# Last combinations in one-bank tiles with copies by block, another place for two steps of the tail, and last logits by blocks

## The chip, the cores and the metric

The kernel runs on one core of one Trainium2 chip. The metric is the device time of one execution in microseconds, lower is better; a time quoted without more is the median of the runs that are not profiled. All data is fp32.

## The reference

A gated linear attention feeds a soft mixture of experts. Cut to what matters:

```python
# q, k, v, f_logit: batch 4, heads 8, 768 tokens, head size 48
f = 1 / (1 + exp(-f_logit))
for t in range(S):
    state = f[:, :, t, :, None] * state + einsum('bhd,bhe->bhde', k[:, :, t], v[:, :, t])
    y[:, :, t] = einsum('bhd,bhde->bhe', q[:, :, t], state)
x = y.transpose(0, 2, 1, 3).reshape(3072, 384)

logits = x @ phi                                   # 3072 tokens x 32 slots (8 experts x 4)
d = softmax of logits over the tokens (axis 0)
slot_input = d.T @ x                               # 32 x 384
slot_out[e] = relu(slot_input[e] @ w1[e]) @ w2[e]  # 384 -> 1024 -> 384, 8 experts
c = softmax of logits over the slots (axis 1)
out = c @ slot_out                                 # 3072 x 384
```

The softmax over the tokens needs the logits of all tokens, so no expert can start before the last token's logits are there; and no output row can be made before the experts are done.

## The kernel before

The attention is done in 12 units of work (`NU`; half of the batch rows times 128 tokens), the mixture in 6 groups of two units (`NV`). Each unit goes through decays (ScalarE, VectorE, GpSimd), scores, mask, and the inner products that make y in transposed form in the PSUM tiles PB[0] and PB[1] (`intra`, L283). ScalarE copies y to SBUF (`y_copy`, L294), TensorE transposes it back (`x_tr`, L299). Once both units of a group have their y, `c_lg` (L317) makes the group's logits, 32 slots x 128 columns for each of four blocks n: blocks 0 and 1 take the group's first unit, blocks 2 and 3 the second, one block for each y copy. A block is 32 columns of TensorE wide and sums over four chunks p. `c_max` keeps a running maximum over the tokens, `c_exp`, `c_tr`, `c_copy` bring the exponentials to the other layout, `c_pin` (L360) pools x with them and `c_join` adds that to the sum with rescaling.

The last group (units 10 and 11) is the bottleneck's end: its logits lie in PC[:, 0], a column behind them (L327, `c_first`) holds the old maximum, so that one reduction (L331) gives the new one. From it a chain of small steps (`t_max`, `c_exp`, `c_pin`, `t_psi`) leads to the pooled inputs of the experts, and `tail` begins: `up` (L423, first weights, ScalarE relu), `turn` (L429, transposes, with a masked VectorE copy L430), `down` (L469, second weights). `down` runs in two parts of the 384 output columns, h = 0 with 256 and h = 1 with 128 columns, 16 steps of four matmuls each. `slot_out` (L476, VectorE) scales the result, `slot_out2` (L481 TensorE, L482 ScalarE's copy to s4) sums it over the experts' copies.

Then come the combinations, `combine(h, y)`, three for each h: combination weights ct times s4 for two groups of tokens. `c_ct(h)` (L463 transposes, L465 copy) brings these weights, softmaxed over the slots, into ct, for h = 0 the first three groups, for h = 1 the last three. A combination makes 8 matmuls L501 in four banks of PSUM, one for each block n of 32 partitions of s4, two groups x each; the copies to SBUF (stage) are ScalarE's L503, for the two banks of a pair at once, and VectorE's L509 (`combine_2`), one for each of the other two. `store` (L513) sends the result out: 1 MB for h = 0, 0.5 MB for h = 1. All stores are issued on SyncE's queue but the last, which ScalarE issues.

PSUM has eight banks here: four single tiles PA[0], PA[1], PB[0], PB[1], and two pairs, PC and PD, each one tile of two banks. The tile layer puts in the semaphore waits, and each engine works in the order in which the program is written. That order comes from a table: `at(t, fn, ...)` gives each step a time in units of T, `run_atoms` sorts by it, and `tail` and `last` are lists written out by hand at the end. The step that the change to `at` touches reads:

```python
    at((NU - 1) * T + 6.1, c_first, NV - 1)
```

In the rows, tile names come in small letters (pa, pb, pc, pd for PA to PD, s for s4, wr also for the stage of the output), and an fp32 matmul is two passes, so 16 products show as x32.

Of the kernel before, what the change touches and what calls it, by code (L numbers as in the profile page):

```python
# [16 lines left out]
NU = 12  # L17
NV = 6
# [5 lines left out]
WC, CO = (256, 128), (0, 256)  # L24
# [20 lines left out]
T = 8.6  # L45
# [12 lines left out]
def gla_soft_moe_kernel(ctx: ExitStack, tc: tile.TileContext, q, k, f, v, vd, phi, w1, w2, out):  # L58
# [9 lines left out]
    nc = tc.nc  # L68
# [3 lines left out]
    def P(shape, name, dt=F32):  # L72
        return pool.tile(shape, dt, tag=name, name=name)
# [6 lines left out]
    def at(t, fn, *args):  # L80
        atoms.append((round(t, 4), len(atoms), fn, args))
# [38 lines left out]
    pin = P([128, DM], "pin")  # L120
# [17 lines left out]
    PA, PB = ([pp.tile([128, 512], F32, tag=f"{n}{w}", name=f"{n}{w}") for w in range(2)] for n in ("pa", "pb"))  # L138
    PC, PD = (pp.tile([128, 2, 512], F32, tag=n, name=n) for n in ("pc", "pd"))
# [168 lines left out]
    def lgs(g):  # L308
        return PA[0][:, :128] if g < NV - 1 else PC[:, 0, :128]
# [1 line left out]
    def trs(g):  # L311
        return PB[0] if g < NV - 2 else PC[:, 1]

    def c_lg(g):
        for p in range(4):
            for n in range(4):
                nc.tensor.matmul(lgs(g)[32 * n : 32 * n + 32], phs[:, p], xTs[2 * g + n // 2][:, n % 2, p], start=p == 0, stop=p == 3)  # L317


# [158 lines left out]
    def slot_out2(h):  # L478
# [4 lines left out]


    FIN = [
        [(PC, PA[0], PA[1]), (PD, PB[1], PA[0]), (PC, PA[1], PB[1])], [(PD, PB[0], PA[1]), (PC, PB[1], PA[0]), (PD, PB[0], PA[1])],
    ]
    stage = [
        wr[:, a:b].rearrange("p a x -> p (a x)").rearrange("p (v n d) -> p v n d", v=NV, n=4) for a, b in ((7, 11), (11, 13))
    ]  # L490

    def combine(h, y, last=(2, 3)):

        hs_, wc = slice(CO[h], CO[h] + WC[h]), WC[h]
        two, b2, b3 = FIN[h][y]
        banks = [two[:, 0], two[:, 1], b2, b3]
        for n2 in range(2):
            for x in range(2):
                for n in (n2, n2 + 2):
                    ns = slice(32 * n, 32 * n + 32)  # L500
                    nc.tensor.matmul(banks[n][:, wc * x : wc * x + wc], ct[ns, 2 * y + x], s4[ns, hs_], start=True, stop=True)  # L501
        dst = stage[h][:, 2 * y : 2 * y + 2]
        nc.scalar.copy(dst[:, :, :2].rearrange("p v n d -> p n v d"), two[:, :, : 2 * wc].rearrange("p n (v d) -> p n v d", v=2))  # L503
        for n in last:
            combine_2(h, y, n)

    def combine_2(h, y, n):
        wc = WC[h]
        nc.vector.tensor_copy(stage[h][:, 2 * y : 2 * y + 2, n], FIN[h][y][n - 1][:, : 2 * wc].rearrange("p (v d) -> p v d", v=2))  # L509

    def store(h, y):
        o, n = 4 * NV * CO[h], 8 * WC[h]
# [35 lines left out]
    STEPS = [(j, kk) for j in range(2) for kk in range(8)]  # L548

    def tail(late):  # L550

        items = [(t_psi,), (c_exp, NV - 1, (1,)), (t_zs,), (up, 0, 0), (up, 0, 1), (up, 1, 0)]
        items += [(c_tr, NV - 1, (1,)), (flag_2,), (c_copy, NV - 1, (1,)), (turn, 0, 0), (turn, 0, 1), (t_z,), (c_soft, 1), (flag_3,), (c_soft2, 1), (up, 1, 1)]
        items += [(load_w2, i, home) for i, home in late]
        items += [(down, 0, *STEPS[x]) for x in range(8)]
        items += [(turn, 1, 0), (turn, 1, 1), (c_ct, 1)]
        items += [(down, 0, *STEPS[x]) for x in range(8, 16)]
        items += [(slot_out, 0)]
        items += [(down, 1, *STEPS[x]) for x in range(3)]
        items += [(slot_out2, 0)]  # L560
        items += [(down, 1, *STEPS[x]) for x in range(3, 7)]
        for y in range(3):
            items += [(combine, 0, y, (2,) if y == 2 else (2, 3))]
            items += [(store, 0, y)] if y < 2 else []
            items += [(down, 1, *STEPS[x]) for x in ((7, 8, 9), (10, 11, 12), (13, 14, 15))[y]]
        items += [(slot_out, 1), (combine_2, 0, 2, 3), (store, 0, 2), (slot_out2, 1), (hint,)]
        for y in range(3):
            items += [(combine, 1, y), (store, 1, y)]
        return items


    o = OFF
# [55 lines left out]
    at((NU - 1) * T + 6.5, flag)  # L628
    at((NU - 2) * T + 6.45, c_soft, 0)
    at((NU - 1) * T + 6.4, c_soft2, 0)  # L630
    at((NU - 1) * T + 6.1, c_first, NV - 1)

    for i in range(16):
        at((1.6 + 0.62 * i) * T - 0.9, load_w1, i)
# [1 line left out]
    def span(name, n=1):  # L636
        off = place[name][0]
        return [arena[:, off + UN * x : off + UN * x + UN] for x in range(n)]

    homes = list(zip(  # L640
        [9 * T + 6.9, 10 * T + 6.9, 10 * T + 4.5, 10 * T + 4.6, 10 * T + 4.0, 11 * T + 4.0, 10 * T + 6.4, 11 * T + 6.4, 12 * T - 0.5],
        span("f", 2) + span("p", 2) + span("k", 2) + span("q", 2) + span("v"),
    ))
    homes.sort(key=lambda a: a[0])
    for i, (t, home) in enumerate(homes):
        at(t, load_w2, i, home)
    spare = span("xT")[0]
# [4 lines left out]
    ending = tail(late)  # L652
    z = NU * T - 0.4
    last = [
        (x_tr, NU - 1, (0,)), (c_lg, NV - 1), (x_tr, NU - 1, (1,)), (load_w2, len(homes) - 1, spare), (x_copy, NU - 1, (0,)), (c_max, NV - 1),
        (t_max,), (c_exp, NV - 1, (0,)), (x_copy, NU - 1, (1,)), (c_tr, NV - 1, (0,)), (c_ct, 0, (0,)), (t_max2,), (c_copy, NV - 1, (0,)), (t_max3,),
        (c_pin, NV - 1), (c_ct, 0, (1,)), (c_join, NV - 1), (warm, 1),
    ]
# [126 lines left out]
```

## Time and profile before

| | us |
|---|---|
| median of 3 runs without profile | 156.45 (156.2 to 156.59) |
| the profiled execution | 155.44 |
| its span, first to last instruction | 153.7 |
| TensorE matmul busy | 138.1 (90%) |
| VectorE, ScalarE, GpSimd busy | 104.3, 94.3, 58.5 |
| DMA | 53.97 MB, mean 351 GB/s over the span |

TensorE is busy nearly all the time up to 140 us. A busy share says little about the tail, though: there the last row of TensorE ends about 9 us before the span does, and the rest is the stores on their way. So the time line around 104 to 112 us (the last group's logits) and 128 to 146 us (the combinations), the issue times of the stores and the DMA share by slices are what is to be read.

### The profile page before, as it was taken

The page shows a single profiled execution, that of the slowest core. Times are in us where ns is not written, and L with a number is a line of the kernel's source. Part 1 is how long each engine was busy: PE and PEld are TensorE (multiplying, and loading weights), DVE is VectorE, ACT ScalarE, POOL GpSimd, SP SyncE. Part 2 cuts the span into 40 slices and gives each one's busy share as a digit, 9 for nine tenths or more (in the row PEclk, how much of TensorE's full clock was granted, in tenths as well). Part 3 has the DMA queues.
Part 4 walks back from the last instruction along what each step waited for, and adds up shares of the span by engine and source line. Part 5 has one row for each costly group of instructions (what it writes and reads, how often), then busy time and mean ns, then how long its engine had stood idle before and what let it go on. Part 6 is the DMA issues. An engine that isn't in the chain of part 4 may idle for free.

```text
span 153.7 us, 5505 instructions
## 1 busy us (share of the span) xinstructions
PE 138.1 (90%) x2392; PEld 109.4 (71%) x2392; DVE 104.3 (68%) x153; ACT 94.3 (61%) x182; POOL 58.5 (38%) x51
## 2 busy tenths in 40 slices
PE   7987999999889999999999999999889999997500
PEld 7976888989769898889879897877433556675400
DVE  6899686999579887896969887759510563146500
ACT  4998899997789796969596976334402121035400
POOL 7008585788556483909293655600000000000000
PEclk9999999999999999999999999999999999999965
DMA  4899999999999999999999939999999993009990
GB/s 153 279 364 421 402 408 406 412 409 411 410 404 415 401 410 398 393 401 389 397 410 406 388 113 374 412 419 420 417 417 337 422 422 156 0 4 420 409 386 32
DMA packets 13424, 53.97 MB, mean 351 GB/s; under 512 B 1488, under 2 KB 1616, under 8 KB 13008
## 3 DMA queue, kind: packets, MB, share of 16 engines
q1 hardware_dynamic: 13248, 53.02, 87.2%
q10 hardware_dynamic: 144, 0.52, 0.9%
q8 instruction: 20, 0.33, 0.9%
q14 instruction: 12, 0.10, 0.2%
HBM read 48.82 MB, written 4.72 MB: 348 GB/s over the span
## 4 chain that ended last, share of the span: by engine, by line


## 5 line engine op out<-in xcount | busy, mean ns | idle before, releaser
L210 POOL TENSOR_TENSOR arena<-arena 128x512 f32<-128x512 f32 (+1 forms) x15 | 28.6, 1908 | 38.9 <-ACT arena L196 28.4
L239 DVE TENSOR_TENSOR arena<-pd,mask 128x1024 f32<-128x1024 f32 x23 | 27.8, 1210 | 10.2 <-PE pd L230 10.2
L193 DVE TENSOR_TENSOR_SCAN arena<-again,arena 128x512 f32<-128x512 f32 (+1 forms) x17 | 30.3, 1787 | 3.3 <-ACT arena L188 3.3
L230 PE MATMUL pd<-arena 48*128 48x128 f32 x368 | 27.0, 285 | 1.6 <-DVE arena L239 0.6
L206 POOL TENSOR_TENSOR arena<-arena 128x512 f32<-128x512 f32 (+1 forms) x15 | 27.6, 1852 | 0.4 <-POOL arena L206 0.4
L230 PEld LDWEIGHTS pd<-arena 48*128 48x128 f32 x368 | 22.3, 187 | 5.7 <-POOL arena L206 1.7
L283 PE MATMUL pb<-arena 128*48 128x128 f32 x384 | 23.5, 274 | 0.0
L283 PEld LDWEIGHTS pb<-arena 128*48 128x48 f32 x384 | 20.3, 123 | 1.1 <-issue 0.8
L196 ACT ACTIVATE arena<-arena 128x512 f32<-128x512 f32 (+1 forms) x17 | 13.6, 801 | 10.5 <-DVE arena L193 10.5
L294 ACT COPY arena<-pb 128x512 f32<-128x512 f32 x24 | 13.6, 584 | 6.6 <-PE pb L283 6.3
L185 ACT ACTIVATE arena<-arena 128x512 f32<-128x512 f32 (+1 forms) x16 | 13.5, 847 | 1.5 <-DMA arena<-in_f_dram 1.5
L202 ACT ACTIVATE arena<-arena 128x512 f32<-128x512 f32 (+1 forms) x17 | 13.8, 811 | 0.3
L188 ACT ACTIVATE arena<-arena 128x512 f32<-128x512 f32 (+1 forms) x16 | 13.5, 844 | 0.5
L299 PE MATMUL pa<-ident,arena 112*128 112x112 f32 x96 | 11.6, 262 | 0.3 <-ACT arena L294 0.3
L274 PE MATMUL pb<-arena 48*48 48x128 f32 x320 | 10.9, 274 | 0.0
L299 PEld LDWEIGHTS pa<-ident,arena 112*128 112x128 f32 x96 | 9.7, 141 | 1.1 <-ACT arena L294 0.7
L252 PE MATMUL pc<-arena 128*48 128x48 f32 x320 | 9.2, 210 | 0.9 <-ACT arena L222 0.9
L252 PEld LDWEIGHTS pc<-arena 128*48 128x48 f32 x320 | 8.1, 125 | 2.6 <-ACT arena L222 1.1
L219 PE MATMUL pc<-ident,arena 112*128 112x112 f32 x80 | 9.9, 266 | 0.0
L274 PEld LDWEIGHTS pb<-arena 48*48 48x48 f32 x320 | 8.4, 119 | 1.4 <-issue 0.2
L219 PEld LDWEIGHTS pc<-ident,arena 112*128 112x128 f32 x80 | 7.8, 141 | 1.9 <-issue 1.0
L165 PE MATMUL pd<-ones 128*128 128x128 f32 x50 | 7.3, 317 | 1.1 <-POOL ones L143 1.1
(140 smaller groups left out, 199.3 us busy)
## 6 DMA issues: line engine op xcount, KB each, us to landing
wr<-in_w_dram SPq DMA_DIRECT2D x22, 768.0 KB, 8.6
arena<-in_w_dram SPq DMA_DIRECT2D x10, 768.0 KB, 9.4
arena<-in_f_dram SPq DMA_DIRECT2D x10, 512.0 KB, 7.4
arena<-in_q_dram SPq DMA_DIRECT2D x10, 512.0 KB, 8.5
arena<-in_k_dram SPq DMA_DIRECT2D x10, 512.0 KB, 7.1
arena<-in_v_dram SPq DMA_DIRECT2D x12, 384.0 KB, 7.3
out_dram<-wr SPq DMA_DIRECT2D x3, 1024.0 KB, 4.8
arena<-in_f_dram SPq DMA_DIRECT2D x4, 256.0 KB, 4.1
```

Of the source, the lines that this page charges most:

```text
L193: nc.vector.tensor_tensor_scan(t, cols(again, h), t, 0.0, op0=ALU.mult, op1=ALU.add)
L196: nc.scalar.activation(cols(R("p", u), h), cols(R("f", u), h), AF.Exp, scale=-1.0)
L202: nc.scalar.activation(cols(G(u), h), cols(R("f", u), h), AF.Exp)
L206: (eng or nc.gpsimd).tensor_tensor(t, t, cols(G(u), h), op=ALU.mult)
L210: (eng or nc.gpsimd).tensor_tensor(t, t, cols(R("p", u), h), op=ALU.mult)
L219: nc.tensor.transpose(PC[:, a // 4, 128 * (a % 4) : 128 * (a % 4) + W], kq[:W, a], ident[:W, :W])
L230: nc.tensor.matmul(t[:, 128 * p : 128 * p + 128], kq[rs, 4 * w + p], qq[rs, 4 * w + p], start=True, stop=True)
L239: nc.vector.tensor_tensor(dst, src, mask.unsqueeze(1).broadcast_to(list(dst.shape)), op=ALU.mult)
L252: nc.tensor.matmul(kvs[64 * r : 64 * r + D, a], kr[:, a, r], vb(u, a, r ^ a // 4), start=True, stop=True)
L274: nc.tensor.matmul(ys[a][o : o + D], heads(S0(u), D)[rs, a], qq[rs, a], start=p == 0, stop=False, skip_group_check=True,)
L283: nc.tensor.matmul(ys[4 * w + p][o : o + D], vb(u, 4 * w + p, r ^ w), sc[:, r, p], start=u < 2 and p == 0, stop=p == 3, skip_group_check=True,
L299: nc.tensor.transpose(PA[w][:, 128 * p : 128 * p + W], xTs[u][:W, w, p], ident[:W, :W])
```

## The change

Four things. The last group's logits are made in two calls of `c_lg`: blocks 0 and 1 (unit 10) behind the pooling of the group before, blocks 2 and 3 (unit 11) where all four stood; `c_first` moves one unit ahead. In `FIN` a combination's four banks are listed one by one, and none takes both banks of PC or PD; the copies go bank by bank, ScalarE blocks 0 and 1, VectorE blocks 2 and 3, in the order 0, 2, 1, 3 (the line is now L503 for both engines, and a store's is L509). `c_ct(1)` stands behind `slot_out(0)` instead of behind the turns. And the combinations of h = 0 stand elsewhere among the steps of `down(1)`: the first behind 2 steps instead of 7, the second behind 7 instead of 10, the third behind all 16 and `slot_out(1)` instead of behind 13.

```diff
-    def c_lg(g):
+    def c_lg(g, blocks=(0, 1, 2, 3)):
         for p in range(4):
-            for n in range(4):
+            for n in blocks:
                 nc.tensor.matmul(lgs(g)[32 * n : 32 * n + 32], phs[:, p], xTs[2 * g + n // 2][:, n % 2, p], start=p == 0, stop=p == 3)

     FIN = [
-        [(PC, PA[0], PA[1]), (PD, PB[1], PA[0]), (PC, PA[1], PB[1])], [(PD, PB[0], PA[1]), (PC, PB[1], PA[0]), (PD, PB[0], PA[1])],
+        [(PC[:, 0], PA[1], PB[1], PD[:, 0]), (PA[0], PC[:, 1], PD[:, 1], PB[1]), (PA[1], PC[:, 0], PD[:, 0], PB[1])],
+        [(PC[:, 1], PA[0], PB[0], PD[:, 1]), (PA[1], PC[:, 0], PB[1], PD[:, 0]), (PA[0], PC[:, 1], PB[0], PD[:, 1])],
     ]
...
-        dst = stage[h][:, 2 * y : 2 * y + 2]
-        nc.scalar.copy(dst[:, :, :2].rearrange("p v n d -> p n v d"), two[:, :, : 2 * wc].rearrange("p n (v d) -> p n v d", v=2))
-        for n in last:
-            combine_2(h, y, n)
-
-    def combine_2(h, y, n):
-        wc = WC[h]
-        nc.vector.tensor_copy(stage[h][:, 2 * y : 2 * y + 2, n], FIN[h][y][n - 1][:, : 2 * wc].rearrange("p (v d) -> p v d", v=2))
+        for n in (0, 2, 1, 3):
+            (nc.scalar.copy if n < 2 else nc.vector.tensor_copy)(
+                stage[h][:, 2 * y : 2 * y + 2, n], banks[n][:, : 2 * wc].rearrange("p (v d) -> p v d", v=2),
+            )
...
-        items += [(turn, 1, 0), (turn, 1, 1), (c_ct, 1)]
+        items += [(turn, 1, 0), (turn, 1, 1)]
         items += [(down, 0, *STEPS[x]) for x in range(8, 16)]
-        items += [(slot_out, 0)]
-        items += [(down, 1, *STEPS[x]) for x in range(3)]
-        items += [(slot_out2, 0)]
-        items += [(down, 1, *STEPS[x]) for x in range(3, 7)]
-        for y in range(3):
-            items += [(combine, 0, y, (2,) if y == 2 else (2, 3))]
-            items += [(store, 0, y)] if y < 2 else []
-            items += [(down, 1, *STEPS[x]) for x in ((7, 8, 9), (10, 11, 12), (13, 14, 15))[y]]
-        items += [(slot_out, 1), (combine_2, 0, 2, 3), (store, 0, 2), (slot_out2, 1), (hint,)]
+        items += [(slot_out, 0), (c_ct, 1), (slot_out2, 0)]
+        items += [(down, 1, *STEPS[x]) for x in range(2)]
+        items += [(combine, 0, 0), (store, 0, 0)]
+        items += [(down, 1, *STEPS[x]) for x in range(2, 7)]
+        items += [(combine, 0, 1), (store, 0, 1)]
+        items += [(down, 1, *STEPS[x]) for x in range(7, 16)]
+        items += [(slot_out, 1), (combine, 0, 2), (slot_out2, 1), (store, 0, 2), (hint,)]
...
-    at((NU - 1) * T + 6.1, c_first, NV - 1)
+    at((NU - 1) * T + o["pin"] - 3 * T + 0.01, c_lg, NV - 1, (0, 1))
+    at((2 * NV - 3) * T + o["mx"] + 0.01, c_first, NV - 1)
...
-        (x_tr, NU - 1, (0,)), (c_lg, NV - 1), (x_tr, NU - 1, (1,)), (load_w2, len(homes) - 1, spare), (x_copy, NU - 1, (0,)), (c_max, NV - 1),
+        (x_tr, NU - 1, (0,)), (c_lg, NV - 1, (2, 3)), (x_tr, NU - 1, (1,)), (load_w2, len(homes) - 1, spare), (x_copy, NU - 1, (0,)), (c_max, NV - 1),
```

What that does to the engines' order shows at three places. The first is TensorE around the last logits (L230 scores, L360 pooling of the group before, L283 inner products of the last unit, L299 its transposes; pa_85, pa_86 are PA[0], PA[1], pb_87, pb_88 are PB[0], PB[1]):

```order
 L230 MATMUL pd<-arena 128x128 x8
 L360 MATMUL pa_86<-arena,el 32x384 x4
-L283 MATMUL pb_87<-arena 48x128 x8
-L283 MATMUL pb_88<-arena 48x128 x8
-L299 MATMUL pa_85<-ident,arena 128x112 x4
-L317 MATMUL pc<-arena,phs 32x128 x16
+L317 MATMUL pc<-arena,phs 32x128 x8
+L283 MATMUL pb_87<-arena 48x128 x8
+L283 MATMUL pb_88<-arena 48x128 x8
+L299 MATMUL pa_85<-ident,arena 128x112 x4
+L317 MATMUL pc<-arena,phs 32x128 x8
```

Eight of the sixteen products went ahead of the inner products; the other eight stayed behind the first transposes.

The second is TensorE from the sum of h = 0 to the second combination, in the changed program, with the semaphores that an instruction waits for (a wait on DVE is one for VectorE, on Activation one for ScalarE):

```order
L501 MATMUL pc<-s_84,ct 128x256 [waits Activation_49]
L501 MATMUL pb_88<-s_84,ct 128x256
L501 MATMUL pc<-s_84,ct 128x256
L501 MATMUL pb_88<-s_84,ct 128x256
L501 MATMUL pa_86<-s_84,ct 128x256
L501 MATMUL pd<-s_84,ct 128x256
L501 MATMUL pa_86<-s_84,ct 128x256
L501 MATMUL pd<-s_84,ct 128x256
L469 MATMUL pb_87<-arena 32x128 x20
L501 MATMUL pa_85<-s_84,ct 128x256
L501 MATMUL pd<-s_84,ct 128x256 [waits DVE_49]
```

The second combination starts 20 products behind the first, and its second instruction, into PD, waits for VectorE once more after the first combination's last product into PD.

The third is ScalarE from the first combination to the copy of the second sum (L482), before and after:

```order
L482 COPY s_84<-pd 128x256
L503 COPY wr<-pc 128x2x2x256
L503 COPY wr<-pd 128x2x2x256
L503 COPY wr<-pc 128x2x2x256
L482 COPY s_84<-pa_85 128x128
```

```order
L482 COPY s_84<-pd 128x256
L503 COPY wr<-pc 128x2x256
L503 COPY wr<-pa_86 128x2x256
L503 COPY wr<-pa_85 128x2x256
L503 COPY wr<-pc 128x2x256
L503 COPY wr<-pa_86 128x2x256
L503 COPY wr<-pc 128x2x256
L482 COPY s_84<-pa_85 128x128
```

Each copy of two banks became two of one bank, and the copy of the second sum still stands behind those of the third combination, which on TensorE now comes after all of `down(1)`.

## Rows read from the trace of the kernel before

**Rows 1.** The page's first line.

```profile
span 153.7 us, 5505 instructions
```

**Rows 2.** Time line, last logits: start us, us, engine line op out<-in xcount [idle before<-releaser].

```profile
103.58 0.85 PE L360 MATMUL pa<-arena,el 128*32 128x384 f32 x8
...
104.36 1.95 PE L283 MATMUL pb<-arena 128*48 128x128 f32 x32
...
106.25 0.60 PE L299 MATMUL pa<-ident,arena 112*128 112x112 f32 x4
106.37 0.58 ACT L294 COPY arena<-pb 128x512 f32<-128x512 f32 x1 [0.29 <-PE pb L283]
...
106.78 1.29 PE L317 MATMUL pc<-arena,phs 128*32 128x128 f32 x32
...
108.11 0.29 DVE L331 TENSOR_REDUCE nmx<-pc 128x1 f32<-128x129 f32 x1 [0.39 <-PE pc L317]
```

**Rows 3.** Time line, TensorE: an earlier group's logits and what follows them.

```profile
95.73 1.06 PE L317 MATMUL pa<-arena,phs 128*32 128x128 f32 x32
...
96.72 1.95 PE L283 MATMUL pb<-arena 128*48 128x128 f32 x32
```

**Rows 4.** Time line: first up product; then windows: stretch, us, busy by engine, PEclk, DMA.

```profile
112.27 2.78 PE L423 MATMUL pa<-wr,et 128*32 128x512 f32 x24 [0.39 <-DVE et L413]
...
112.50:120.00 7.50, 7.50 (x72) 2.08 (x64) 0.00 (x0) 1.19 (x2) 0.00 (x0) 1.00 0.98 376
```

**Rows 5.** Time line around the second turn of the combine weights.

```profile
128.35 0.69 DVE L430 TENSOR_TENSOR arena<-pb,emask 128x512 f32<-128x512 f32 x1 [2.51 <-PE pb L429]
...
128.59 0.49 PE L463 MATMUL pa<-ident,el 128*128 128x128 f32 x3
...
129.10 0.11 PEld L469 LDWEIGHTS pd<-arena 128*32 128x32 f32 x2 [0.26 <-DVE arena L430]
```

**Rows 6.** Time line: first two combinations; the first row is a pair of single-bank copies on ScalarE.

```profile
99.61 1.05 ACT L294 COPY arena<-pb 128x512 f32<-128x512 f32 x2
...
134.00 1.08 PE L469 MATMUL pb<-arena 128*32 128x128 f32 x32
134.10 0.37 ACT L482 COPY s<-pd 128x256 f32<-128x256 f32 x1 [4.51 <-PE pd L481]
...
135.01 0.48 PE L501 MATMUL pc<-s,ct 32*128 32x256 f32 x1
...
136.19 1.29 DVE L509 COPY wr<-pa 128x512 f32<-128x512 f32 x2 [2.88 <-PE pa L501]
...
136.26 1.01 ACT L503 COPY wr<-pc 128x1024 f32<-128x1024 f32 x1 [1.79 <-PE pa L501]
...
136.89 0.48 PE L501 MATMUL pd<-s,ct 32*128 32x256 f32 x1
...
137.99 0.30 PE L469 MATMUL pb<-arena 128*32 128x128 f32 x2
```

**Rows 7.** Time line, issues of the first three stores (SyncE) and the last (ScalarE).

```profile
137.54 0.35 SPq L513 DMA_DIRECT2D out_dram<-wr  x1
...
139.42 0.34 SPq L513 DMA_DIRECT2D out_dram<-wr  x1
...
141.82 0.33 SPq L513 DMA_DIRECT2D out_dram<-wr  x1
...
145.12 0.38 ACTq L513 DMA_DIRECT2D out_dram<-wr  x1
```

**Rows 8.** Windows of the store traffic: the last two columns are DMA share and GB/s.

```profile
138.30:138.40 0.10, 0.10 (x14) 0.10 (x8) 0.10 (x1) 0.10 (x1) 0.00 (x0) 1.00 0.81 328
...
138.50:149.75 11.25, 4.80 (x106) 3.43 (x94) 4.67 (x11) 3.59 (x6) 0.00 (x0) 0.90 1.00 404
149.75:150.25 0.50, 0.00 (x0) 0.00 (x0) 0.00 (x0) 0.00 (x0) 0.00 (x0) 0.50 0.29 115
...
151.00:151.75 0.75, 0.00 (x0) 0.00 (x0) 0.00 (x0) 0.00 (x0) 0.00 (x0) 0.50 0.05 22
```

More of the change, by code (lines that the diff above doesn't have):

```diff
@@ L490, in gla_soft_moe_kernel, with combine @@
     ]
-    def combine(h, y, last=(2, 3)):
+    def combine(h, y):
         hs_, wc = slice(CO[h], CO[h] + WC[h]), WC[h]
-        two, b2, b3 = FIN[h][y]
-        banks = [two[:, 0], two[:, 1], b2, b3]
+        banks = FIN[h][y]
         for n2 in range(2):
```

## The prediction

> **What bounds the kernel now.** I read the time line of the two stretches that the change touches, then the issue times of the stores, then the DMA share of the last 16 us in slices. The profiled execution took 155.44 us, of which the span from first to last instruction is 153.7 [rows 1]; 1.74 us lie around it. The median of the runs without a profile is 156.45, 1.01 us above. I work out a difference against the profiled execution and add it to the median.
>
> Three things set the end, one after the other. First, TensorE around 104 to 108 us: the second-last group's pooling (L360) is followed without a pause by the last unit's inner products (L283, 104.36, 1.95 us), the transposes (L299, 106.25) and the last logits (L317, 106.78) [rows 2]. VectorE's maximum (L331, 108.11) waits for the logits, and a chain of small steps leads from it to the up products, which wait 0.39 us for its last step at 112.27 and then keep TensorE busy for every microsecond of 112.5 to 120 [rows 2, 4]. From there TensorE goes on without slack: whatever delays the maximum delays the first store. Second, the first store: it is issued at 137.54 and its data begins in the slice 138.30 to 138.40, so 0.8 us later [rows 7, 8]. Third, the store traffic: from 138.5 to 149.75 the 16 DMA engines are busy all the time at 404 GB/s, then most stop, and a few go on until about 151.7 [rows 8]. The six stores carry 4.72 MB, and 4.72 MB at 404 GB/s is 11.7 us. So the end is the start of the first store's data plus a fixed amount of traffic, as long as no later store comes too late.
>
> **Part 1, last logits by blocks.** The 16 products of the last group are cut in two: blocks 0 and 1 (unit 10) now stand ahead of the last unit's inner products, and only blocks 2 and 3 (unit 11) stay at 106.78. The cost hangs on how TensorE runs four blocks of 32 columns. An earlier group's 32 passes take 1.06 us at 273 ns each, so eight run at once on average counting their latency, and the next kind of product starts 0.99 us after the first pass [rows 3]. That is eight rounds of four passes: (1.06 - 0.27) / 7 = 0.11 us a round. The four blocks run side by side, and each has eight passes of its own (four chunks, two passes for each fp32 product). Two blocks therefore also take eight rounds, 8 x 0.11 = 0.88 us.
>
> What does it save at 106.78? Block 3 needs the second copy of unit 11, which ends at 106.37 + 0.58 = 106.95; its eight rounds from there end at 106.95 + 0.05 + 7 x 0.11 + 0.27 = 108.04, which is when the row of L317 ends (106.78 + 1.29 = 108.07) [rows 2]. So block 3 alone sets the end of the logits, and taking blocks 0 and 1 away saves nothing there. What does it cost at 104.3? TensorE has no pause there: L360's row ends at 104.43, L283's begins at 104.36 and ends at 106.31, L299's begins at 106.25 [rows 2]. The early half pushes all of that back. Bounds: 0 if it ran beside its neighbours, 0.99 by the earlier group's row; I take 0.87, since it follows products of the same width and so adds no second change of shape. The stopgap column of the maximum (L327, 0.15 us on VectorE) also moves forward, ahead of work that VectorE finishes before TensorE needs it, and is costed at nothing; if that cover were gone it would cost 0.15.
>
> **Part 2, the second turn of the combine weights** (three transposes L463 and ScalarE's copy L465). Before, it stood ahead of the second half of the down products. Those wait for VectorE's masked copy (128.35 + 0.69 = 129.04) and start at 129.10 with 0.26 us idle after the turn [rows 5], so the turn was hidden and taking it away gains nothing. Its new place is after the last down product of the first part, while VectorE scales the result; 0.49 us fit into that stretch, which 12 products of the next part filled before. TensorE's sum still waits for VectorE and comes at the same time; ScalarE's copy (about 0.48 us) is over before the sum's copy at 134.10 is due [rows 6]. Cost zero.
>
> **Part 3, first combination earlier.** 28 down products of the second part stood ahead of it; now there are 8. Its input is ready at 134.10 + 0.37 = 134.47. Before, 16 products ran from 134.00 and it started at 135.01; with 8 of them, four rounds of 0.11 fewer, it starts at 134.57. Everything behind it comes 0.43 to 0.44 us earlier. Its copies: VectorE still has two of 512 columns, 1.29 us together; ScalarE's one copy of 1024 (1.01) becomes two of 512, which take 1.05 together at 99.61 [rows 6]. VectorE ends last as before, so copies by block neither help nor hurt the first store. It is issued at 137.54 - 0.43 = 137.11 on the old clock (all times of parts 3 and 4 leave out part 1's shift).
>
> **Part 4, what comes behind.** Second combination: TensorE reaches it after 20 products at 136.89, as before [rows 6]. But in the changed program's order its product into the second bank of PD waits for VectorE, and the only thing of PD that VectorE still has to read is the first combination's copy out of the first bank, which is VectorE's second and ends at 135.76 + 1.29 = 137.05. So it starts at 137.10, 0.21 late; queued behind it on TensorE are the rest of the combination and nine steps of down products, and the second store waits for it: 139.42 + 0.21 = 139.63. In the Trainium skill, "PSUM — Partial Sum Buffer", section "PSUM bank collisions raise a hardware error", different banks may be read and written at once; by that the wait would not be needed and the 0.21 would be gone, but no run here shows it, and the program has the wait.
>
> Third combination: it now stands behind all nine steps (18 rounds of 0.11) instead of three. From 137.99 + 0.21: down products to about 140.2, combination from 140.3, copies from 141.5 to 142.8, store issued at 142.85, against 141.82 before [rows 7]: 1.03 us later. ScalarE's copy of the second sum now queues behind two copies of this combination and ends near 142.9, so the last three stores are issued 0.9 to 1.6 us later, the last at about 146.7 instead of 145.12 [rows 7].
>
> Does the traffic notice? Two stores of 1.05 MB at 404 GB/s last 5.19 us: from 137.92 to 143.11. The third store's data can begin 0.8 us after its issue, at 143.65 to 143.70. The engines then pause for 0.55 us. The last three stores are issued at least 0.9 us before the traffic reaches them and cost nothing. For an engine that keeps up, the sum of the tail is -0.43 + 0.57 = +0.14. For the few that lag at the end, and whose end is the end [rows 8], the pause is partly or wholly filled by the work they are behind with: down to -0.43. I take -0.1, between the two, nearer to the engines that keep up at that moment. In the Trainium skill, "DMA: Bandwidth & Descriptors", section "Latency and other measured facts", the first byte comes after about 600 ns. The rows here show 0.8; by the page the pause would be 0.2 shorter and the tail some 0.1 to 0.2 better.
>
> **Sum.** +0.87 - 0.1 = +0.77 us: 156.2 in a profile, and 156.45 + 0.77 = 157.2 as a median.
>
> **Rivals.** (A) The lagging engines swallow the pause, so the tail gives its full 0.43: +0.87 - 0.43 = +0.44, 156.9. For it: the drip after 149.75 is long, 1.9 us [rows 8]. Against it: most of that lag seems to arise in the second half of the traffic. (B) The early half of the logits costs nothing, because TensorE runs it in columns that its neighbours leave idle; then the tail alone counts: -0.1, 156.35, or -0.43 with A, 156.0. This decides once the early half costs less than 0.57. Against it: the inner products before and after fill both halves of the columns, and TensorE has no pause from 103.6 on. (C) The pause is longer: if the wait on PD holds back more than 0.21, or the copies of the third combination, now on both engines while the sum's copy waits, take 0.3 more, the third store's data begins at 144.0 and no engine can fill the pause: +0.87 + 0.14 + 0.3 = +1.3, 157.75.
>
> **How the numbers follow.** About 0.3%, 0.47 us, is what a measurement of this kernel can tell from no change: 155.98 to 156.92. Forecast 0.52, A 0.2, B 0.08, C 0.2. The forecast's own spread is 156.95 to 157.5. Faster needs B with the whole tail: 0.04. Same: the rest of B, more than half of A, and the low edge of the forecast: 0.22. Slower: 0.74. The range reaches from the lower part of A to C: 156.5 to 157.75, leaving out B and the far side of C.
>
> **What would show it.** Right: the last unit's inner products start near 105.2 instead of 104.36, the maximum near 109.0, the up products near 113.1, the first store is issued near 138.0 (0.4 later than before, not 0.9), the third near 143.7, and the DMA share has a dip of about half a microsecond near 144. Wrong: inner products that still start by 104.5 (B), no dip (A), a dip over 0.8 us (C), or a last logits row much shorter than 1.1 us, which would say that the number of blocks does count.

## The result and the profile after

The changed kernel takes 157.49 us (157.38 to 157.62), the kernel before 156.32 (156.04 to 156.59) beside it: ratio 1.0075, 95% interval 1.0054 to 1.0096, so 1.17 us slower. The prediction was 157.2 in a range of 156.5 to 157.75. In a later comparison the changed kernel came to 1.0064 (1.0036 to 1.0093).

The profiled execution took 157.62 us, against 155.44 before; its page begins:

```profile
span 155.9 us, 5511 instructions
```

Of those 2.2 us, 0.66 lie ahead of everything that the change touches: the pooling of the second-last group (L360) begins at 104.24 instead of 103.58, and one of the first loads lands that much later too (the fifth, at 8.62 instead of 7.97). The pooling's start moves from run to run, between 103.6 and 104.7 over all profiles below. So stages are compared from the pooling on, not from zero.

**The head.** The time line of the changed kernel around the last logits, to be read against [rows 2] (start us, us, engine, line, operation, count, idle before):

```profile
104.24 0.85 PE L360 MATMUL pa<-arena,el 128*32 128x384 f32 x8
...
104.91 1.04 PE L317 MATMUL pc<-arena,phs 128*32 128x128 f32 x16
...
105.88 1.96 PE L283 MATMUL pb<-arena 128*48 128x128 f32 x32
...
108.30 1.29 PE L317 MATMUL pc<-arena,phs 128*32 128x128 f32 x16
...
109.62 0.29 DVE L331 TENSOR_REDUCE nmx<-pc 128x1 f32<-128x129 f32 x1 [1.31 <-PE pc L317]
```

The inner products (L283) start 1.64 us behind the pooling's start instead of 0.78. The second half of the logits, with half the products, takes the same 1.29 us as all of them did. So the maximum stands 5.39 us (5.386 before the rows are rounded) behind the pooling's start instead of 4.53: 0.86 lost, and nothing saved.

**The first store.** From the maximum on, the path is the one of before; this is its time line around the first two combinations, with the stores' issues (SPq, ACTq), to be read against [rows 5 to 7]:

```profile
134.20 0.55 PE L463 MATMUL pa<-ident,el 128*128 128x128 f32 x3
134.34 0.48 DVE L476 TENSOR_SCALAR sob<-pd,small 128x256 f32<-128x256 f32 x1 [3.19 <-PE pd L469]
134.79 0.48 ACT L465 COPY ct<-pa 128x384 f32<-128x384 f32 x1 [8.33 <-PE pa L463]
...
134.88 0.70 PE L481 MATMUL pd<-sob,same 128*128 128x256 f32 x2
...
135.62 0.37 ACT L482 COPY s<-pd 128x256 f32<-128x256 f32 x1 [0.35 <-PE pd L481]
...
136.08 0.48 PE L501 MATMUL pc<-s,ct 32*128 32x256 f32 x1
136.09 0.48 PE L501 MATMUL pb<-s,ct 32*128 32x256 f32 x1
136.11 0.48 PE L501 MATMUL pa<-s,ct 32*128 32x256 f32 x1
136.12 0.48 PE L501 MATMUL pd<-s,ct 32*128 32x256 f32 x1
...
137.90 0.68 DVE L503 COPY wr<-pd 128x512 f32<-128x512 f32 x1
...
138.40 0.48 PE L501 MATMUL pa<-s,ct 32*128 32x256 f32 x1
138.63 0.48 PE L501 MATMUL pd<-s,ct 32*128 32x256 f32 x1
...
138.64 0.35 SPq L509 DMA_DIRECT2D out_dram<-wr  x1
...
141.15 0.34 SPq L509 DMA_DIRECT2D out_dram<-wr  x1
...
144.38 0.33 SPq L509 DMA_DIRECT2D out_dram<-wr  x1
...
148.34 0.38 ACTq L509 DMA_DIRECT2D out_dram<-wr  x1
```

The first store is issued 29.02 us behind the maximum (138.64 - 109.62) instead of 29.43: 0.41 gained. The second combination's product into PD waits to 138.63, just behind VectorE's copy out of PD's other bank (137.90 + 0.68 = 138.58), and the second store comes 2.51 us behind the first instead of 1.88. The third comes 5.74 behind it instead of 4.28.

**The traffic.** Windows of the changed kernel (stretch, us, busy by engine, TensorE clock, DMA share, GB/s), to be read against [rows 8]:

```profile
138.60:139.50 0.90, 0.90 (x16) 0.79 (x15) 0.00 (x0) 0.00 (x0) 0.00 (x0) 1.00 0.00 0
139.50:144.25 4.75, 3.90 (x97) 2.96 (x90) 2.86 (x5) 2.32 (x5) 0.00 (x0) 1.00 1.03 416
144.25:144.50 0.25, 0.22 (x5) 0.22 (x9) 0.07 (x1) 0.00 (x0) 0.00 (x0) 1.00 0.86 360
144.50:145.25 0.75, 0.75 (x24) 0.75 (x20) 0.18 (x1) 0.23 (x1) 0.00 (x0) 1.00 0.25 98
145.25:151.50 6.25, 2.32 (x28) 1.62 (x24) 2.08 (x6) 1.72 (x6) 0.00 (x0) 0.73 1.00 397
151.50:152.25 0.75, 0.00 (x0) 0.00 (x0) 0.00 (x0) 0.00 (x0) 0.00 (x0) 0.50 0.51 175
```

The data of two stores is through at 144.25, the third store's data begins 0.87 us behind its issue at 144.38, and in between the engines lose 0.25 x 0.14 + 0.75 x 0.75 = 0.60 us. Data start 139.50, 11.7 us of traffic and 0.60 of pause end at 151.8, which is where the share falls.

This dip is a low reading: the share of 1.03 ahead of it counts packets whole that run into it, and it is a mean over all engines, of which one may work on through it. The landings tell it more sharply. Each store lands (reports that its data has arrived) in 16 parts, whose times the trace has. The middle ones (the median of the 16), counted from the first issue:

| store | 1 | 2 | 3 | 4 | 5 | 6 | last part of all |
|---|---|---|---|---|---|---|---|
| kernel before | 3.81 | 6.30 | 8.81 | 10.11 | 11.41 | 12.67 | 14.57 |
| changed kernel | 3.83 | 6.31 | 9.54 | 10.83 | 12.12 | 13.42 | 15.65 |

From the third store on the middle parts are 0.71 to 0.75 later and stay so. The last part of all comes about 2 us behind the middle ones in both kernels.

### The profile page after: what moved, and what is told of

Read it like the earlier page. It is cut to its first block, busy times and chain, and to the rows that moved or that the text cites. A ratio compares the mean times of both kernels' runs of the same rounds, so it can differ in the third digit from the quotient of the medians.

```text
span 155.9 us, 5511 instructions
## 1 busy us (share of the span) xinstructions
PE 140.6 (90%) x2392; PEld 111.7 (72%) x2392; DVE 104.3 (67%) x153; ACT 94.8 (61%) x188; POOL 58.4 (37%) x51
## 4 chain that ended last, share of the span: by engine, by line
PE 64%; DVE 11%; DMA 9%; ACT 4%; issue 3%; SPq 2%; POOL 2%; POOLq 0%; DVEq 0%; ACTq 0%
PE pd L230 11%; PE pb L283 8%; DMA arena<-in_q_dram 5%; PE pd L469 5%; PE pb L274 5%; PE pa L299 4%; DVE arena L193 4%; DMA arena<-in_f_dram 4%; PE pc L219 4%; PE pc L252 4%; PE pa L423 3%; PE pb L423 3%; PE pa L360 3%; PE pb L469 3%; PE pa L317 2%
## 5 line engine op out<-in xcount | busy, mean ns | idle before, releaser
L230 PE MATMUL pd<-arena 48*128 48x128 f32 x368 | 27.0, 285 | 1.4 <-DVE arena L239 0.8
L230 PEld LDWEIGHTS pd<-arena 48*128 48x128 f32 x368 | 22.3, 187 | 5.5 <-DVE arena L239 1.8
L283 PE MATMUL pb<-arena 128*48 128x128 f32 x384 | 23.5, 274 | 0.0
L283 PEld LDWEIGHTS pb<-arena 128*48 128x48 f32 x384 | 20.3, 123 | 0.6 <-issue 0.4
L299 PE MATMUL pa<-ident,arena 112*128 112x112 f32 x96 | 11.6, 262 | 0.3 <-ACT arena L294 0.3
L299 PEld LDWEIGHTS pa<-ident,arena 112*128 112x128 f32 x96 | 9.7, 141 | 1.1 <-ACT arena L294 0.7
```

The source lines that it names most:

```text
L230: nc.tensor.matmul(t[:, 128 * p : 128 * p + 128], kq[rs, 4 * w + p], qq[rs, 4 * w + p], start=True, stop=True)
L283: nc.tensor.matmul(ys[4 * w + p][o : o + D], vb(u, 4 * w + p, r ^ w), sc[:, r, p], start=u < 2 and p == 0, stop=p == 3, skip_group_check=True,
L299: nc.tensor.transpose(PA[w][:, 128 * p : 128 * p + W], xTs[u][:W, w, p], ident[:W, :W])
```

## The experiments

Each kernel was timed beside the kernel before. The table has the ratio with its interval, and from each profile the stages: pooling's start to maximum, maximum to first issue, first issue to the end of the span, and what the DMA share lost before the last store's data began (from windows, as above). Spans are printed to 0.1 us, so the column "to the end" holds to 0.05. A row's name is the heading of its section below.

| kernel | ratio | pooling to maximum | to first issue | to the end | dip |
|---|---|---|---|---|---|
| before | 1 | 4.53 | 29.43 | 16.16 | 0 |
| changed | 1.0075 (1.0054 to 1.0096) | 5.39 | 29.02 | 17.26 | 0.60 |
| changed, again | 1.0064 (1.0036 to 1.0093) | 5.39 | 29.03 | 16.97 | 0.65 |
| whole logits | 1.0019 (0.9996 to 1.0042) | 4.53 | 29.02 | 16.91 | 0.56 |
| split alone | 1.0095 (1.0057 to 1.0133) | 5.39 | 29.44 | 16.98 | 0 |
| split alone, again | 1.0091 (1.0058 to 1.0124) | 5.39 | 29.43 | 16.18 | 0 |
| one block early | 1.0110 (1.0056 to 1.0164) | 5.38 | 29.43 | 16.19 | 0 |
| pair banks | 1.0089 (1.0060 to 1.0119) | 5.39 | 28.99 | 17.13 | 0.41 |
| third early | 0.9992 (0.9968 to 1.0017) | 4.53 | 29.02 | 16.25 | 0.30 |
| third early, pair banks | 0.9975 (0.9945 to 1.0004) | 4.53 | 29.00 | 16.40 | 0 |
| first store in halves | 0.9959 (0.9933 to 0.9985) | 4.53 | 28.47 | 16.58 | 0.41 |
| halves, second form | 0.9961 (0.9938 to 0.9984) | 4.53 | 28.47 | 16.51 | 0.32 |

The theory at the start: the early half of the logits costs 0.86 us because TensorE has no pause there (H), the earlier first combination gives back 0.41, and the pause ahead of the third store costs its length again (P). The rivals: the head's delay is absorbed (B), or a lagging DMA engine fills the pause, so that it costs nothing (L).

### Whole logits

```diff
-    at((NU - 1) * T + o["pin"] - 3 * T + 0.01, c_lg, NV - 1, (0, 1))
-    at((2 * NV - 3) * T + o["mx"] + 0.01, c_first, NV - 1)
+    at((NU - 1) * T + 6.1, c_first, NV - 1)
...
-        (x_tr, NU - 1, (0,)), (c_lg, NV - 1, (2, 3)), (x_tr, NU - 1, (1,)), (load_w2, len(homes) - 1, spare), (x_copy, NU - 1, (0,)), (c_max, NV - 1),
+        (x_tr, NU - 1, (0,)), (c_lg, NV - 1), (x_tr, NU - 1, (1,)), (load_w2, len(homes) - 1, spare), (x_copy, NU - 1, (0,)), (c_max, NV - 1),
```

> The changed kernel with one part undone: the last group's logits stand whole in their old place again, all 16 products behind the first transposes of the last unit, and the column for the maximum in its old place. Theory H (the early half of the logits delays the inner products by its whole length, and block 3 alone sets the end of the logits): inner products start some 0.8 us after the pooling instead of 1.64, maximum, first store and end 0.86 us earlier, so 157.49 - 0.86 = 156.6 (156.4 to 156.85). What is left over the kernel before (156.32) is then the tail's share, +0.3. Rival B (the head is absorbed before the stores, and the whole difference comes from the tail): 157.3 to 157.5, while the maximum comes earlier.

Measured 156.33, a ratio of 1.0019 against 1.0075 and 1.0064 for the changed kernel: 0.7 to 0.9 us of the loss are gone. The 156.33 lies just under the expected 156.4 to 156.85, but the kernel before took 156.04 beside it instead of 156.32; the ratio is the expected one. In its time line everything is back:

```profile
104.04 0.85 PE L360 MATMUL pa<-arena,el 128*32 128x384 f32 x8
...
104.83 1.96 PE L283 MATMUL pb<-arena 128*48 128x128 f32 x32
...
107.24 1.29 PE L317 MATMUL pc<-arena,phs 128*32 128x128 f32 x32
108.57 0.29 DVE L331 TENSOR_REDUCE nmx<-pc 128x1 f32<-128x129 f32 x1 [0.39 <-PE pc L317]
```

The maximum stands 4.53 us behind the pooling's start, as before. B falls. What remains over the kernel before is the tail: 0.41 earlier at the first issue, 0.75 longer from there.

### Split alone, and again

To the kernel before, only the lines of the last diff the other way round, with `c_lg` taking its blocks.

> The kernel before with one part of the change alone: the last logits in two halves, and the column for the maximum moved with them; combinations, copies and the turn of the weights as before. Theory H: maximum and first store 0.86 us later, and nothing behind them reacts, so 156.32 + 0.86 = 157.2 (156.95 to 157.4). Rival B (absorbed): 156.2 to 156.5. If it comes out above 157.4, the later start meets something else in the store traffic.

> The kernel before with the split logits alone, run again, since its first comparison (1.0095, interval 1.0057 to 1.0133, six runs) lies above the 0.86 us that its trace shows between pooling and maximum. Theory H: 1.0055 (0.86 us), with 14.6 us from the first store's issue to the last landing as in the kernel before. Rival: a late start of the tail costs another 0.5 us behind the last landing, ratio 1.009 again.

The time line of the second run:

```profile
103.61 0.85 PE L360 MATMUL pa<-arena,el 128*32 128x384 f32 x8
...
105.25 1.95 PE L283 MATMUL pb<-arena 128*48 128x128 f32 x32
...
108.99 0.29 DVE L331 TENSOR_REDUCE nmx<-pc 128x1 f32<-128x129 f32 x1 [1.31 <-PE pc L317]
```

The traces say H to the hundredth: maximum 5.39 behind the pooling's start, everything up to the last landing as before (14.68 and 14.57 us behind the first issue, 14.57 in the kernel before), and in the second run, whose pooling starts at the same time as that of [rows 2] (103.61 and 103.58), a profiled execution of 156.32 against 155.44. But the runs without a profile say 1.0095 and 1.0091, 1.4 to 1.5 us, with the lower ends of the intervals at 0.9; the first median, 157.70, is above the expected 157.4. In the first run's profile 0.7 us of excess can be seen: the span ends 2.3 us behind the last store's landing instead of 1.6, with a late fetch of instructions in between. The second shows none of it. Some may lie ahead of the pooling: it starts at 104.21 in the mean of the six profiles with split logits and at 103.84 in that of the six without; whether that is the split or scatter was not tested. So H's price is shown by the traces and by the kernel with whole logits; why the runs without a profile of this kernel lie another half microsecond higher stays open, and by medians alone the parts do not add up (1.4 for the split, 0.3 for the tail, 1.0 to 1.2 for both).

### One block early

To the kernel with the split alone:

```diff
-    at((NU - 1) * T + o["pin"] - 3 * T + 0.01, c_lg, NV - 1, (0, 1))
+    at((NU - 1) * T + o["pin"] - 3 * T + 0.01, c_lg, NV - 1, (0,))
```

and `(1, 2, 3)` instead of `(2, 3)` for the call that stays behind.

> The kernel before, with only block 0 of the last group's logits in the early place instead of blocks 0 and 1 (4 products instead of 8), and blocks 1 to 3 at the old place. If TensorE's time goes by rounds and the blocks run side by side, one block costs as much as two: inner products 0.86 us later than in the kernel before (1.64 us behind the pooling's start), the maximum too, time 156.04 + 0.86 = 156.9. If it goes by products, half: inner products 1.21 us behind the pooling's start, maximum 0.43 later, 156.5.

Its time line around the last logits:

```profile
104.70 0.85 PE L360 MATMUL pa<-arena,el 128*32 128x384 f32 x8
105.37 1.04 PE L317 MATMUL pc<-arena,phs 128*32 128x128 f32 x8
106.33 1.96 PE L283 MATMUL pb<-arena 128*48 128x128 f32 x32
...
108.75 1.29 PE L317 MATMUL pc<-arena,phs 128*32 128x128 f32 x24
```

Four products in one block of columns hold the inner products back as long as eight in two (0.96 us from L317's start to L283's; 0.97 above), so what is paid for here is rounds, not blocks. The 12 that stay take 1.29 us like 16, but there block 3, whose y copy is the last to come, sets the end. Its median, from four runs, 158.06 against an expected 156.9, is high like that of the split alone.

### Pair banks

```diff
-        [(PC[:, 0], PA[1], PB[1], PD[:, 0]), (PA[0], PC[:, 1], PD[:, 1], PB[1]), (PA[1], PC[:, 0], PD[:, 0], PB[1])],
+        [(PC[:, 0], PC[:, 1], PA[0], PA[1]), (PD[:, 0], PD[:, 1], PB[1], PA[0]), (PC[:, 0], PC[:, 1], PA[1], PB[1])],
...
```

> The changed kernel with the list of banks of the kernel before: blocks 0 and 1 of a combination in both banks of PC or of PD, so that no pair is shared by neighbouring combinations; copies still bank by bank, logits and order as changed. Theory W (the second combination is held by the wait on PD for the first combination's last VectorE copy): the second store is issued about 2.3 us after the first instead of 2.51, the third 0.2 earlier too, and the pause of the DMA engines is 0.2 shorter. With theory P (the pause costs its length): 157.3. With rival L (a lagging engine fills the pause): 157.4 to 157.5 in spite of the earlier stores. If the second store still comes 2.5 us after the first, the wait was not the cause.

The first three issues in its time line, and the window of its dip:

```profile
138.27 0.35 SPq L509 DMA_DIRECT2D out_dram<-wr  x1
...
140.59 0.34 SPq L509 DMA_DIRECT2D out_dram<-wr  x1
...
143.78 0.33 SPq L509 DMA_DIRECT2D out_dram<-wr  x1
```

```profile
144.00:144.75 0.75, 0.75 (x30) 0.75 (x30) 0.19 (x1) 0.11 (x1) 0.00 (x0) 1.00 0.46 186
```

The second store comes 2.32 us behind the first, the third 5.51, and the dip is 0.75 x 0.54 = 0.41: the wait was the shared pair, and it cost 0.2. The middle parts of the last store land 0.2 us sooner behind the first issue than in the changed kernel (13.19 against 13.42). The ratio, 1.0089 (1.0060 to 1.0119), shows no gain, and P's 157.3 and L's 157.4 to 157.5 are both within its interval, so this kernel does not decide between them.

### Third combination early

To the kernel with whole logits:

```diff
-        items += [(down, 1, *STEPS[x]) for x in range(7, 16)]
-        items += [(slot_out, 1), (combine, 0, 2), (slot_out2, 1), (store, 0, 2), (hint,)]
+        items += [(down, 1, *STEPS[x]) for x in range(7, 11)]
+        items += [(combine, 0, 2), (store, 0, 2)]
+        items += [(down, 1, *STEPS[x]) for x in range(11, 16)]
+        items += [(slot_out, 1), (slot_out2, 1), (hint,)]
```

> The kernel with whole logits (first of this series), and besides the third combination and its store moved from behind all 16 steps of the second part of the down products to behind 11 of them; banks and copies as in the changed kernel. The third store should be issued some 1.2 to 1.5 us sooner after the first than in the changed kernel (5.74 us there), well before the traffic of the first two is through (5.2 us after the first data), so no pause of the DMA engines. Theory P (the pause of about 0.6 us costs its length at the end): 0.4 to 0.6 below the kernel with whole logits, about 156.1, and 0.2 to 0.4 below the kernel before. Rival L (the end is set by a DMA engine that lags anyway and fills the pause with its own backlog): no change against the kernel with whole logits, 156.5 to 156.7.

Windows of its store traffic:

```profile
138.25:145.50 7.25, 6.41 (x133) 4.99 (x130) 4.01 (x8) 3.26 (x8) 0.00 (x0) 1.00 1.00 409
145.50:146.00 0.50, 0.28 (x11) 0.09 (x4) 0.24 (x1) 0.44 (x2) 0.00 (x0) 1.00 0.40 156
146.00:149.75 3.75, 0.95 (x8) 0.76 (x8) 0.94 (x3) 0.58 (x2) 0.00 (x0) 0.68 1.00 392
```

155.89, 0.44 us under the kernel with whole logits, as P expected (the means of the two kernels, timed side by side, differ by 0.5, give or take 0.4). The third store comes 4.65 us behind the first, 1.1 sooner rather than 1.2 to 1.5. The pause ahead of it is gone, but a smaller one, 0.5 x 0.6 = 0.30 us, stands ahead of the fourth, which now comes 7.78 behind the first: TensorE waits in this kernel at the second and third combination for copies out of shared pairs (0.23 us at the second, 137.01 to 137.24 between its first two blocks). From first issue to the end it is 16.25, within 0.1 of the kernel before. Against that kernel the ratio of 0.9992 is no difference that can be measured, where P expected 0.2 to 0.4 us.

This smaller pause did not cost its length at the end, and that speaks for L: the middle parts of the last store land 12.93 us behind the first issue, 0.26 later than in the kernel before, but its last part 14.61, only 0.04 later. One part was late all along here (the last parts of the six stores land at 6.08, 8.50, 10.93, 12.27, 13.38 and 14.61); that it belongs to one engine, which filled the pause with its backlog and set the end, fits these times but is not shown. So P holds for the pause ahead of the third store, and not for this one. (How large this dip is depends on where the windows are cut; the next expectation has it at 0.17.)

### Third early and pair banks

Whole logits, the third combination behind 11 steps, and the banks of the kernel with pair banks.

> The kernel with whole logits and the third combination behind 11 steps, and besides the list of banks of the kernel before, so that neighbouring combinations share no pair. In the kernel with the third combination early TensorE lost some 0.4 us on waits for copies out of shared pairs, and the fourth store was issued 7.78 us after the first, so late that the DMA share dipped for 0.17 us at 8.3 to 8.8 us after the first issue. Expected here: second store 2.3 us after the first, fourth by 7.5, no dip at all, and of the whole tail only the earlier first combination is left: 0.41 under the kernel before, a ratio of 0.9974 (0.996 to 0.999). Rival (a 16 KB block of instructions that now comes after the first store's data has begun, 1 us behind its issue instead of 0.4 ahead of it, makes one DMA engine late by 2 us, and that engine sets the end): the gain is eaten, ratio 0.999 to 1.002, with the last store landing more than 14.9 us after the first issue.

Windows of its store traffic:

```profile
138.85:150.00 11.15, 5.63 (x138) 4.26 (x126) 4.91 (x11) 4.15 (x11) 0.00 (x0) 0.87 1.01 406
150.00:150.25 0.25, 0.00 (x0) 0.00 (x0) 0.00 (x0) 0.00 (x0) 0.00 (x0) 0.50 0.33 131
```

The share is full from the first store's data to 150.00 without a dip, the fourth store comes 7.17 behind the first, and from first issue to the last landing it is 14.59 us against 14.57 in the kernel before. The ratio of 0.9975 is the one expected (0.9974), though the interval reaches just past 1, so the gain is seen in the trace and not secured by the runs. The rival named here fell too: the 16 KB block of instructions was indeed fetched behind the first issue, and the first store's last part landed 5.75 us behind its issue instead of 3.96, but the end did not move.

### First store in halves

To the last kernel: the first combination's copies go by group of tokens, with a store of 0.5 MB behind each half, and the later combinations stand two steps further ahead.

```diff
+        for x in range(parts):
...
+            for n in (0, 2, 1, 3):
+                (nc.scalar.copy if n < 2 else nc.vector.tensor_copy)(
+                    stage[h][:, g, n], banks[n][:, c].rearrange("p (v d) -> p v d", d=wc),
+                )
...
-        items += [(combine, 0, 0), (store, 0, 0)]
-        items += [(down, 1, *STEPS[x]) for x in range(2, 7)]
+        items += [(combine, 0, 0, 2), (store, 0, 0, 2)]
+        items += [(down, 1, *STEPS[x]) for x in range(2, 5)]
```

> The kernel with whole logits, pair banks and the third combination early, and besides the first combination's copies made by group of tokens instead of all at once, with a store of 0.5 MB behind each half; the second and third combination two steps further forward, so that their stores are there in time. If the end is the start of the first store's data plus a fixed 11.7 us of traffic as long as no later store comes too late, the first issue comes 0.5 us sooner than in the kernel without halves (1.26 us of copies become 0.75 for the first half) and the end with it: ratio to the kernel before 0.994 (0.992 to 0.996). Rival (the TensorE chain of 16 steps and three combinations now sets when the fourth store is issued, and the DMA engines pause ahead of it instead): a dip of up to 0.4 us, ratio 0.996 to 0.998.

> The kernel with the first store in halves, with the second combination behind 6 steps instead of 5 and the third still behind 9. In its first form the second combination's block 3 waited some 0.4 us on TensorE for VectorE's copies of the second half, all steps behind it were late by that, the fourth store came 8.11 us after the first and the DMA share dipped for 0.4 us. Expected: the step in between fills half of that wait, second store unchanged (2.4 us after the first), fourth store near 7.9, the dip 0.2 us or gone, time 0.2 us under the first form, a ratio of 0.9945 to 0.996. Rival: TensorE's wait stays as long and the dip with it; no difference from the first form (0.9959).

The second form has the second combination behind 6 steps. The first issue comes 0.53 us sooner in both, and both are faster than the kernel before: 155.70 us, 0.9959 (0.9933 to 0.9985), and 155.36, 0.9961 (0.9938 to 0.9984). Against the kernel without halves (0.9975) no difference is secured. The rival took part of the gain: the last part of the last store lands 14.76 us behind the first issue in the first form and 14.99 in the second, against 14.59 without halves. Windows of the first form:

```profile
137.75:145.25 7.50, 6.41 (x155) 4.90 (x154) 4.07 (x9) 3.47 (x9) 0.00 (x0) 1.00 1.01 409
145.25:145.75 0.50, 0.38 (x16) 0.19 (x8) 0.38 (x2) 0.16 (x2) 0.00 (x0) 1.00 0.18 66
```

The engines lose 0.5 x 0.82 = 0.41 us ahead of the fourth store, issued 8.11 us behind the first; 7.89 in the second form, as expected, with a dip of 0.32, more than the 0.2 expected; its second store comes 2.63 us behind the first instead of 2.41. Between the two forms no difference shows. By that dip it is the fourth store that is late there now, the first of h = 1, which waits for the down products of h = 1.

### The changed kernel again

> The changed kernel itself, for a comparison on the same chip and in the same hour as the others of this series: 1.0075 of the kernel before, first store to last landing 15.2 to 15.7 us, a dip of 0.6 us between the data of the second and the third store. If that stretch comes out near 15.2, the excess of its first profile over 14.57 (kernel before) plus the dip of 0.61 was scatter; if again near 15.7, something besides the dip costs 0.4 us.

First issue to last landing 15.42 us (15.65 in the first profile), dip 0.65. So the late third store costs 0.85 to 1.08 at the landing where the dip is 0.60 to 0.65; in the kernel with whole logits it is 0.77 for 0.56, and with pair banks 0.58 for 0.41. Part of this excess is the low reading of the dip: the middle parts of the last store land 0.75, 0.75, 0.77 and 0.52 later than in the kernel before. The rest, 0.0 to 0.3, is how far the last part trails the middle ones, and that varies between three profiles of the same tail (1.90, 2.00 and 2.23 us); why was not tested.

## Why the prediction was right, and which term was off

- **Part 1, +0.87: right.** 0.86 in the trace of every kernel with the split, by the mechanism given: rounds, no pause on TensorE, and block 3 alone at the end.
- **Part 2, zero: right.** Turn and copy of the weights (134.20, 134.79) run while VectorE scales (L476) and TensorE sums (L481); the sum's copy stands 30.53 us behind the pooling's start with the turn in its old place and in its new one (kernel before, and whole logits).
- **Part 3, -0.43: right**, -0.41. The copies by block did neither good nor harm to the first store.
- **Part 4, the wait on PD, 0.21: right**, 2.51 against 2.32 with other banks. By the Trainium skill, "PSUM — Partial Sum Buffer", section "PSUM bank collisions raise a hardware error", two different banks need no such wait; the program has it, because the pair is one tile. No run here writes one bank of a pair while the other is read, so the rule itself is not shown; the cure was another choice of banks.
- **Part 4, third store 1.03 later and a pause of 0.55: right in mechanism, the pause too short.** The store came 1.05 later (5.74 - 4.28 - 0.41). The pause is 0.60 by the windows and 0.73 by the middle parts: a store of 1.05 MB takes them 2.50 us (3.81 to 6.31), not the 2.60 of 404 GB/s, which is the mean over a stretch with engines that lag, so two stores are through 0.19 sooner. In the Trainium skill, "DMA: Bandwidth & Descriptors", section "Latency and other measured facts", the first byte comes after some 600 ns; here it came 0.87 us behind the start of the issue (which itself takes 0.35), and the measurement decides. By that figure the pause would not have come out shorter, as the prediction has it, since the first store's data would begin sooner by as much as the third's.
- **The term that was mis-sized is the tail's sum, taken as -0.1.** I had it between -0.43 (lagging engines fill the pause) and +0.14 (they do not), and leaned to the lag. By the kernel with whole logits, which is this tail alone, it is -0.41 + 0.75 = +0.34, and 0.86 + 0.34 = 1.20 us: the measured 1.17 (1.00 in the later comparison). Of the 0.44 that were missing, 0.24 are the lag that I credited and 0.16 the pause, 0.73 instead of the 0.57 of that sum. The pause did not vanish: from the first issue to the end the changed kernel takes 0.8 to 1.1 us more, and the two kernels without a pause ahead of the third store (third early, with and without pair banks) take 0.1 to 0.25 more. The lag that I counted on is there at that moment in one part alone: of the second store's 16 parts one lands at 8.24 us behind the first issue, the others from 6.23 to 6.67. Most of the lag that sets the end arises later (the last store's parts land from 13.35 to 15.65), as my own argument against A had it, so it could not fill a pause ahead of the third store. In the kernel with no pause the same early lag costs nothing (14.59 against 14.57 us).
- **Rivals.** A (the pause is swallowed) fell for this pause, by the kernel with whole logits and the one with the third combination early; the smaller and later pause of the latter was swallowed, 0.26 us in the middle parts and 0.04 at the end. B fell with whole logits. C had the sign of the miss, but not its cause: the wait on PD and the third store's issue were as forecast, and the pause is longer because the first two stores were through sooner.
- **Luck.** The median of 157.49 is within 0.3 us of the forecast, less than the split kernels' runs without a profile lie above their traces; what bears the forecast out is its parts in the traces (the head, the first store, the wait on PD, the third store's issue), not that number.

## What to carry to other kernels

Before moving half of a step forward, ask whether the engine has a pause at the new place and whether the remaining half gets shorter; work in side-by-side column blocks got no shorter here when a block left it. When the end is a fixed amount of store traffic, list for every store the time by which it must be issued (first data plus the bytes ahead of it, less the 0.87 us to its own first data); an earlier first store moves all these deadlines forward, and a store that misses its own can give the gain back (0.41 gained and 0.77 to 1.08 lost at the last landing here). Before you credit a lagging DMA engine with swallowing a pause, look whether the lag that sets the end is already there at the pause: ahead of the third store one part of 16 was behind, and the pause cost its length; ahead of the fourth, pauses of 0.30 to 0.41 us cost 0.04 to 0.42.

## What the runs showed of the hardware

- By the start times of the profile TensorE does not start small products strictly in the order of the program when they use different rows. In the program the first combination's products go pc, pb, pc, pb, pa, pd, pa, pd; in the rows above pc, pb, pa and pd start at 136.08, 136.09, 136.11 and 136.12, ahead of the second products into pc and pb.
- A block of 32 columns that runs alone takes about as long as two or four side by side: 0.96 us until the next kind of product starts for 4 products in one block, 0.97 for 8 in two, 0.99 for 16 in four [rows 3].
- A fetch of instructions can hold up one part of a store, as if both went through one DMA engine. In the changed kernel a 16 KB block of instructions began 1.06 us behind the first issue and took 1.48 us; the store's last part landed 5.81 us behind its issue, 1.85 later than before, and the other 15 by 4.12 (3.88 before). In the kernel without a pause (third early and pair banks), which has the same delay, it cost nothing at the end.
